# Retention and gated feed-forward on one core: outputs and the new state's transpose in one product of 192 columns

## The chip, the core and the metric

The kernel runs on one core of a Trainium2 chip. The engines of a core work side by side: TensorE (PE) multiplies matrices and writes to PSUM, VectorE (DVE) and ScalarE (ACT) work elementwise on SBUF and PSUM, GpSimd (POOL) works elementwise on SBUF alone in this kernel, and SyncE (SP) issues most of the transfers from and to DRAM. They wait for one another by semaphores. The metric is the device time of one execution in microseconds; the kernel before took 1027.68 us in the median of three runs (1027.46 to 1027.72).

## The reference

Eight batches, eight heads, 576 tokens, 64 channels per head. The first part is retention, that is attention without softmax and with a decay by distance; the second is a feed-forward block on its result.

```python
# q, k, v: (8, 8, 576, 64)
scores = q @ k.T / sqrt(64)
gamma = 1 - 2 ** (-5 - arange(8))                  # one per head
ret = scores * (gamma ** (i - j) if i >= j else 0)
attn = ret @ v
# x: attn as (4608, 512); w_in (512, 2048), w_out (2048, 512)
h = x @ w_in
g = h * erf(softplus(h))
out = g @ w_out
```

q, k, v and the result are float32; w_in and w_out come as float64 and are brought to float32 by the kernel.

## The kernel before

**Attention in pieces.** The 4608 tokens are cut into 36 pieces of 128. A batch has four pieces of 128 tokens and a rest of 64; the rests of two batches make one piece. So pieces 8, 17, 26 and 35 hold two rests, and all others belong to one batch; pieces 0, 4, 9, 13, 18, 22, 27 and 31 begin a batch. Four pieces are one chunk of 512 tokens for the feed-forward part.

The decay is split: the value of token j is weighed with gamma^-j (GpSimd, `weigh_values`), the result of token i with gamma^i, when it is taken out of PSUM. Earlier pieces of the same batch come in by a state, the 64x64 matrix k^T v of each head, summed over the pieces and decayed. Heads lie in pairs: pair p holds heads 2p and 2p+1, one in partitions 0 to 63 and one in 64 to 127 (`heads[e]`).

One piece goes through three stages: `transposes` brings q and k to the channel-by-token layout (by TensorE and ScalarE for early pieces, by VectorE for later ones), `scores` makes q k^T and masks it, and `outputs` makes the result and the new state:

```python
def outputs(i):
    segments = pieces[i]
    t = live.pop(i)
    seen = [(kept[b], r0, n) for b, s0, n, r0 in segments if s0 > 0]
    b, s0, n, _ = segments[0]
    o = [ps_at.tile([P, NP, P], FP32, tag="at", name=f"o{j}") for j in range(2)]
    for p in range(NP):                               # scores times values: L365
        for e in range(2):
            nc.tensor.matmul(
                o[p % 2][heads[(e + p) % 2], p // 2, :],
                lhsT=t["v"][:, 2 * p + e, :],
                rhs=t["sT"][:, e, p, :],
                ...
            )
    for state, r0, m in seen:                         # state times q: L376
        for p in range(NP):
            for e in range(2):
                nc.tensor.matmul(
                    o[p % 2][heads[(e + p) % 2], p // 2, r0 : r0 + m],
                    lhsT=state[heads[e], p, :],
                    rhs=t["qT"][heads[e], p, r0 : r0 + m],
                    ...
                )
    if n == P:                                        # keys times values: L388
        kv = flat(o[0])[:, 2 * P :].rearrange("p (a d) -> p a d", a=NP)
        for p in range(NP):
            for e in range(2):
                nc.tensor.matmul(
                    kv[heads[e], p, :],
                    lhsT=t["k"][:, 2 * p + e, :],
                    rhs=t["v"][:, 2 * p + e, :],
                    ...
                )
    # ... (cut: x's tile, the function scaled)
    scaled(1)                                         # VectorE: out of PSUM, times gamma^i
    if n == P:
        sums = kv
        if s0 > 0:
            sums = att.tile([P, NP, D], FP32, tag="sums", name="sums")
            tt(sums, kv, kept[b], ALU.add)            # VectorE
        # ... (cut: new, a tile)
        (nc.gpsimd if s0 > 0 else nc.vector).tensor_tensor(out=new, in0=sums, in1=gp, op=ALU.mult)
        kept[b] = new
    scaled(0)
    load(i + 3, "kv")
    if i + 1 >= SQUARES:
        weigh_values(i + 1)
```

With (e + p) % 2, the two heads of an odd pair lie in exchanged halves of the result; the order of w_in's rows makes up for it.

**Feed-forward part.** It runs in four passes (g) over groups of the 2048 inner columns, and in each over nine chunks (c). Both matrix products of a chunk are done in the manner of Strassen's method: seven products (`A11`, `A12`, `S2`, `S3`, `S1`, `S4`, `A22`) in place of eight, at the cost of sums of x, of the weights and of the results. One of those products is four matmuls of 256 columns:

```python
def product(self, a, acc, start):
    for j in range(GP):
        for d in range(2):
            nc.tensor.matmul(acc[:, j * TH : (j + 1) * TH],
                lhsT=weights["wa", self.g][:, a, d, j * P : (j + 1) * P],
                rhs=x[self.g, self.c][a][:, d, :], ...)
```

Chunks 0 and 1 of the first pass do the first product without this, in `plain()`: 32 matmuls of 256 columns, which need neither sums of x nor of weights.

**Order.** The program order of all engines is fixed by the kernel: between the products of the feed-forward part, `attend` issues one more stage of the attention, and `round_weights` issues the next step of converting the weights from their double-precision bits to float32. Before the first loads are there, `keep_busy` issues idle products of a tile of ones.

Of the kernel before, what the change touches and what calls it, by code (L numbers as in the profile page):

```python
# [2 lines left out]

# [28 lines left out]
def decays():  # L32
# [7 lines left out]
    out = np.where(np.arange(NP) % 2 == 0, row, np.roll(row, D, axis=0))  # L40
    t = np.arange(P)
    parts = []
    for n in (P, D):
# [3 lines left out]
        gq = out[:, :, None] ** i[None, None, :] / math.sqrt(D)  # L47
# [7 lines left out]
def kernel(  # L55
# [66 lines left out]

    def load_squares(i, name, src):
# [12 lines left out]
    def load_rows(i, name, src, bufs):  # L136
        if name == "q":
            t = raw.tile([P, NP, P * D // SQ], FP32, tag="qs", name="raw_q", bufs=bufs)
            t = t.rearrange("p a x -> p (a x)")[:, : H * D].rearrange("p (h d) -> p h d", h=H)
        else:  # L140
            t = raw.tile([P, H, D], FP32, tag=name, name=f"raw_{name}", bufs=bufs)
# [22 lines left out]
    ones = cpool.tile([P, P], FP32, name="ones")  # L164
    nc.vector.memset(ones, 1.0)
# [26 lines left out]
    def parts():  # L192

        w2 = w_in.rearrange("(e c d) (h f) -> c e d h f", c=n_dc, d=D, h=2)
        for g in range(n_g):
            for dc in range(n_dc):
                a = A11 if dc < 2 else A12
                src = [(heads[(e + dc) % 2], w2[dc, e, :, :, 2 * g * GW : 2 * (g + 1) * GW]) for e in range(2)]

                yield src, "wa", g, a, dc % 2, ["wa"] if g > 0 and dc == n_dc - 1 else []  # L200
            for f in range(2):
                for j in range(GP):
                    ft = f * FH // P + g * GP + j
                    src = [(slice(0, P), w_out[ft * P : (ft + 1) * P, :].rearrange("p (h o) -> p h o", h=2))]
                    sums = (["wb"] if g > 0 else ["wb", "wa"]) if (f, j) == (1, GP - 1) else []
# [97 lines left out]
    kept = {}  # L303
    weighed = set()

# [9 lines left out]
    def transposes(i):  # L315
        t = live[i] = loaded.pop(i)
        if i < SQUARES:
# [23 lines left out]
    def scores(i):  # L341
        t = live[i]
        sT = t["sT"] = att.tile([P, 2, NP, P], FP32, tag="sT", name="sT")
# [10 lines left out]
    def outputs(i):  # L354
        segments = pieces[i]
        t = live.pop(i)
# [3 lines left out]

        b, s0, n, _ = segments[0]
        o = [ps_at.tile([P, NP, P], FP32, tag="at", name=f"o{j}") for j in range(2)]
        for p in range(NP):
            for e in range(2):
                nc.tensor.matmul(  # L365
                    o[p % 2][heads[(e + p) % 2], p // 2, :],
                    lhsT=t["v"][:, 2 * p + e, :],
                    rhs=t["sT"][:, e, p, :],
# [4 lines left out]
        for state, r0, m in seen:  # L373
            for p in range(NP):
                for e in range(2):
                    nc.tensor.matmul(  # L376
                        o[p % 2][heads[(e + p) % 2], p // 2, r0 : r0 + m],
                        lhsT=state[heads[e], p, :],
                        rhs=t["qT"][heads[e], p, r0 : r0 + m],
# [4 lines left out]
        if n == P:  # L384
            kv = flat(o[0])[:, 2 * P :].rearrange("p (a d) -> p a d", a=NP)
# [14 lines left out]
        def scaled(j):  # L400
            to = x[0, c][:, j:NP:2, at : at + P]
            if c < n_ch - 1:
                by = (gq if n == P else gq2)[:, j::2, :].unsqueeze(2).to_broadcast([P, 2, P // n, n])
                dst, got = (y.rearrange("p a (m i) -> p a m i", i=n) for y in (to, o[j][:, :2]))
# [3 lines left out]
            for r0 in range(0, P, n):  # L408
# [3 lines left out]
                    for y in (o[j][:, :2, r0 : r0 + n], (gq if n == P else gq2)[:, j::2, :])  # L412
# [4 lines left out]
        if n == P:  # L417
            sums = kv
            if s0 > 0:
                sums = att.tile([P, NP, D], FP32, tag="sums", name="sums")  # L420
                tt(sums, kv, kept[b], ALU.add)

            if b % 2 == 0 and s0 + P + D == S:
                new = att.tile([P, NP, D], FP32, tag="last", name="last", bufs=1)
            else:
                new = att.tile([P, NP, D], FP32, tag="state", name="state")
# [3 lines left out]
        load(i + 3, "kv")  # L430
# [27 lines left out]
    PLAIN = 2  # L458
# [276 lines left out]
    def keep_busy(n):  # L735
        for _ in range(n):
            nc.tensor.matmul(idle[:, :P], lhsT=ones, rhs=ones, start=True, stop=True)
# [16 lines left out]
    for what in "alkakakawkakakawwaa3awa2aaa5ppppaa5wwppa5ppawappwcppa5ppaaapp5s":  # L754
# [18 lines left out]
    store_x(1)  # L773
    for step, _ in enumerate(firsts[1].plain()):
        if step % 2 == 0:
            attend(min(done[0] + 1, most[0]))
        round_weights(int(step > 1))
        if step == 1:
            firsts[0].softplus()
            firsts[0].erf()  # L780
        elif step == 5:
            firsts[0].multiply()
        elif step == 8:
# [80 lines left out]
```

## Time and profile before

| | |
|---|---|
| time, median of 3 runs | 1027.68 us |
| span of the profiled execution | 1024.0 us |
| granted TensorE clock | 1.000 |
| last attention product | at about 314 us |
| HBM read, written | 117.52 MB, 47.19 MB |

Shares of the engines by stretch of the span, from the busy time of each:

| stretch, us | PE | DVE | ACT | POOL | DMA engines |
|---|---|---|---|---|---|
| 28 to 60 | 97% | 70% | 36% | 25% | 95% |
| 110 to 200 | 100% | 75% | 29% | 20% | 95% |
| 200 to 310 | 100% | 80% | 33% | 25% | 90% |
| 310 to 490 | 100% | 62% | 43% | 11% | 44% |
| 490 to 1024 | 99% | 60% | 39% | 5% | 40% |

A group of the profile is named by its line of the kernel, engine, operation and tiles (`o<-sT,raw_v`: written tile, read tiles), with the part of the array that it uses (`128*64`: 128 rows, 64 columns), partitions by elements, and the count; behind the bar stand the busy time in us, the mean duration of one in ns, and the idle time in front with what ended it. A float32 matmul of the program is two instructions in the trace (for a transpose, one). Line 99 is the helper `tt`, that is all elementwise work of VectorE on two tensors.

### The profile page before, as it was taken

What the parts mean: (1) busy time and instruction counts of PE and PEld (TensorE: products, weight loads), DVE (VectorE), ACT (ScalarE), POOL (GpSimd) and SP (SyncE); (2) the same over time, 40 slices, a digit from 0 to 9 for tenths busy, and PEclk for the clock granted to TensorE, in tenths of its full rate; (3) what the DMA queues carried; (4) which work ended last, traced back from release to release, by engine and by line L of the source; (5) the groups of instructions that cost most, each with busy time, mean ns of one, the idle gap of its engine ahead of it and who ended that gap; (6) DMA issues with size and microseconds to landing.
All of it is one profiled execution on the core that took longest, in us unless ns stands there. A gap on an engine that the chain in (4) does not pass through costs nothing.

```text
span 1024.0 us, 15958 instructions
## 1 busy us (share of the span) xinstructions
PE 1017.6 (99%) x6348; PEld 876.0 (86%) x6348; DVE 667.6 (65%) x1062; ACT 390.2 (38%) x481; POOL 122.6 (12%) x122
## 2 busy tenths in 40 slices
PE   9999999999999999999999999999999999999998
PEld 8787888888888888888888888888888888888887
DVE  3769777976976656656666666666567655555555
ACT  3354134234134444334343444444433333333332
POOL 2143112122312110010001001000100000000000
PEclk9999999999999999999999999999999999999999
DMA  9998989979974354544444345444433333444434
GB/s 200 203 242 175 232 203 223 255 150 253 244 195 150 106 161 145 165 160 154 164 147 158 124 147 162 165 144 144 144 124 124 124 131 127 131 136 131 126 88 119
DMA packets 146986, 165.76 MB, mean 162 GB/s; under 512 B 97376, under 2 KB 121568, under 8 KB 138848
## 3 DMA queue, kind: packets, MB, share of 16 engines
q1 hardware_dynamic: 144832, 163.57, 56.4%
q10 hardware_dynamic: 2080, 1.18, 0.5%
q8 instruction: 50, 0.82, 0.4%
q14 instruction: 24, 0.20, 0.1%
HBM read 117.52 MB, written 47.19 MB: 161 GB/s over the span
## 4 chain that ended last, share of the span: by engine, by line
PE 94%; DMA 3%; DVE 2%; SPq 1%; POOL 1%; issue 0%; ACTq 0%; DVEq 0%; POOLq 0%
PE a L604 24%; PE a L496 23%; PE g L604 12%; PE g L496 12%; PE e L496 6%; PE e L604 6%; PE o L365 3%; PE s L347 3%; PE o L388 2%; DMA raw_k<-in_k_dram 1%; PE o L376 1%; DMA raw_v<-in_v_dram 1%; PE f L668 1%; SPq L147 1%; PE p L550 1%; PE h L668 1%
## 5 line engine op out<-in xcount | busy, mean ns | idle before, releaser
L496 PE MATMUL a<-x,wa 128*128 128x256 f32 x1088 | 258.3, 380 | 0.0
L496 PEld LDWEIGHTS a<-x,wa 128*128 128x128 f32 x1088 | 205.7, 190 | 28.5
L604 PE MATMUL a<-wb,s 128*128 128x256 f32 x840 | 200.0, 381 | 0.0
L604 PEld LDWEIGHTS a<-wb,s 128*128 128x128 f32 x840 | 158.4, 190 | 22.9 <-ACT o L618 0.7
L99 DVE TENSOR_TENSOR t<-g,t 128x512 f32<-128x512 f32 x68 | 47.0, 691 | 151.9 <-ACT t L526 114.1
L496 PE MATMUL g<-x,wa 128*128 128x256 f32 x544 | 129.2, 380 | 0.0
L496 PEld LDWEIGHTS g<-x,wa 128*128 128x128 f32 x544 | 102.8, 190 | 14.4
L99 DVE TENSOR_TENSOR o<-a,o 128x512 f32<-128x512 f32 x104 | 71.4, 687 | 46.4 <-PE a L604 46.4
L521 ACT COPY t<-a 128x512 f32<-128x512 f32 x34 | 19.9, 586 | 188.3 <-PE a L496 188.3
L99 DVE TENSOR_TENSOR t<-t,s 128x1024 f32<-128x1024 f32 x72 | 88.4, 1267 | 0.0
L274 POOL TENSOR_TENSOR wraw<-wraw 128x512 f32<-128x512 f32 x28 | 29.4, 1051 | 438.1 <-DVE wraw L272 184.4
L565 ACT ACTIVATE s<-t 128x1024 f32<-128x1024 f32 x72 | 72.1, 1049 | 24.6 <-DVE t L99 24.5
L99 DVE TENSOR_TENSOR x<-x 128x512 f32<-128x512 f32 x115 | 75.8, 693 | 1.2
L532 ACT COPY t<-a 128x512 f32<-128x512 f32 x34 | 19.9, 586 | 144.4 <-PE a L496 144.4
L569 ACT ACTIVATE s<-s 128x1024 f32<-128x1024 f32 x72 | 72.1, 1049 | 0.4
L604 PE MATMUL g<-wb,s 128*128 128x256 f32 x280 | 66.7, 381 | 0.0
L604 PE MATMUL e<-wb,t 128*128 128x256 f32 x280 | 66.6, 380 | 0.0
L604 PE MATMUL a<-wb,t 128*128 128x256 f32 x280 | 66.6, 380 | 0.0
L604 PE MATMUL g<-wb,t 128*128 128x256 f32 x280 | 66.4, 380 | 0.0
L99 DVE TENSOR_TENSOR sT<-s,cst 128x512 f32<-128x512 f32 x72 | 46.2, 682 | 30.4 <-PE s L347 30.4
L496 PE MATMUL e<-x,wa 128*128 128x256 f32 x272 | 64.8, 381 | 0.0
L99 DVE TENSOR_TENSOR o<-g,o 128x512 f32<-128x512 f32 x70 | 47.9, 684 | 20.9 <-ACT o L618 18.1
(86 smaller groups left out, 1247.1 us busy)
## 6 DMA issues: line engine op xcount, KB each, us to landing
od<-o SPq DMA_DIRECT2D x54, 512.0 KB, 3.3
x<-xd SPq DMA_DIRECT2D x27, 1024.0 KB, 4.8
o<-od SPq DMA_DIRECT2D x27, 1024.0 KB, 5.4
raw_qs<-in_q_dram SPq DMA_DIRECT2D x96, 112.0 KB, 4.4
raw_ks<-in_k_dram SPq DMA_DIRECT2D x84, 112.0 KB, 4.2
xd<-x SPq DMA_DIRECT2D x9, 1024.0 KB, 5.2
raw_v<-in_v_dram SPq DMA_DIRECT2D x64, 128.0 KB, 4.5
wraw<-in_moe_w_in_dram SPq DMA_DIRECT2D x32, 256.0 KB, 5.7
```

The lines of the kernel that those rows point to most:

```text
L99: nc.vector.tensor_tensor(out=out, in0=in0, in1=in1, op=op)
L274: engine.tensor_tensor(out=r_f, in0=high_f, in1=r_f, op=ALU.mult)
L347: nc.tensor.matmul(ps[e][:, p, :], lhsT=t["kT"][heads[e], p, :], rhs=t["qT"][heads[e], p, :], start=True, stop=True)
L365: nc.tensor.matmul(o[p % 2][heads[(e + p) % 2], p // 2, :], lhsT=t["v"][:, 2 * p + e, :], rhs=t["sT"][:, e, p, :], start=(p < 2), stop=(no ...
L388: nc.tensor.matmul(kv[heads[e], p, :], lhsT=t["k"][:, 2 * p + e, :], rhs=t["v"][:, 2 * p + e, :], start=False, stop=(p == NP - 1), skip_gr ...
L496: nc.tensor.matmul(acc[:, j * TH : (j + 1) * TH], lhsT=weights["wa", self.g][:, a, d, j * P : (j + 1) * P], rhs=x[self.g, self.c][a][:, d, :],
L521: nc.scalar.copy(out=self.t1[:, 1], in_=self.a)
L532: nc.scalar.copy(out=self.t2[:, 0], in_=self.a)
L565: nc.scalar.activation(self.s[:, j], t, AF.Softplus)
L569: nc.scalar.activation(self.s[:, j], self.s[:, j], AF.Erf)
L604: nc.tensor.matmul(acc[:, tp, :], lhsT=left[:, j * TH + tp * P : j * TH + (tp + 1) * P], rhs=weights["wb", self.g][:, b, j, :], start=(sta ...
L668: nc.tensor.matmul(acc, lhsT=left[:, j * TH + tp * P : j * TH + (tp + 1) * P], rhs=weights["wb", self.g][:, b, j, :], start=(b in (B11, B2 ...
```

## The change

Five things go together.

1. From piece 13 on, in pieces of one batch, masked scores and keys of a head lie side by side in one tile, `keys`, 128 and 64 columns. One product with the values as the stationary operand gives the outputs in 128 columns and v^T k, the transpose of the new state's share, in 64 more. The separate products of keys and values go for those pieces.
2. That share comes out of PSUM by VectorE's transpose, which turns blocks of 32x32. GpSimd adds and decays; ScalarE puts the off-diagonal blocks of each head in their places (`place_state`).
3. The state is written into a tile `whole`, as a block-diagonal 128x128 matrix for each pair. State times q of both heads of a pair is then one product of 128x128 and not two of 64x64. For this, head e must lie in half e of the result, so (e + p) % 2 becomes e, for all pieces; w_in's rows follow.
4. Keys as rows now live in the tile `keys`; for pieces from 13 on they are loaded for two pieces ahead, where it was three; those of 13 and 14 are loaded at the end of piece 12.
5. Chunk 1 of the first pass does its first product by seven products, like later chunks. The order around it is changed accordingly, and the sums of the weights wa of the first pass are issued earlier.

The tile of ones for the idle products goes; they read `whole`, which is set to zero at first.

```diff
+    BESIDE = 13
+    WIDE = P + D
+    keys = att.tile([P, 3, H * WIDE], FP32, name="keys", bufs=1)
...
+    whole = cpool.tile([P, NP, P], FP32, name="whole")
+    nc.vector.memset(whole, 0.0)
...
+    def place_state():
+        while unplaced:
+            dst, src = unplaced.pop()
+            for e in range(2):
+                for a in range(2):
+                    rows, to = (slice(e * D + x * SQ, e * D + (x + 1) * SQ) for x in (a, 1 - a))
+                    cols = (e * D if dst is whole else 0) + a * SQ
+                    nc.scalar.copy(
+                        out=dst[to, :, cols : cols + SQ], in_=src[rows, :, (1 - a) * SQ : (2 - a) * SQ]
+                    )
...
     def outputs(i):
+        place_state()
+        wide = n == P and i >= BESIDE
         for p in range(NP):
             for e in range(2):
+                h = 2 * p + e
                 nc.tensor.matmul(
-                    o[p % 2][heads[(e + p) % 2], p // 2, :],
-                    lhsT=t["v"][:, 2 * p + e, :],
-                    rhs=t["sT"][:, e, p, :],
+                    o[p % 2][heads[e], p // 2, : WIDE if wide else P],
+                    lhsT=t["v"][:, h, :],
+                    rhs=beside(i)[:, h, :] if wide else t["sT"][:, e, p, :],
...
         for state, r0, m in seen:
             for p in range(NP):
+                dst, by = o[p % 2][:, p // 2, r0 : r0 + m], t["qT"][:, p, r0 : r0 + m]
+                if state is whole and n == P:
+                    nc.tensor.matmul(
+                        dst, lhsT=whole[:, p, :], rhs=by, start=False, stop=(p >= NP - 2), skip_group_check=True
+                    )
+                    continue
                 for e in range(2):
                     nc.tensor.matmul(
-                        o[p % 2][heads[(e + p) % 2], p // 2, r0 : r0 + m],
-                        lhsT=state[heads[e], p, :],
-                        rhs=t["qT"][heads[e], p, r0 : r0 + m],
+                        dst[heads[e]],
+                        lhsT=state[heads[e], p, heads[e] if state is whole else slice(0, D)],
+                        rhs=by[heads[e]],
...
-        if n == P:
+        if n == P and not wide:
             ... (keys times values)
...
+        if wide:
+            sums = att.tile([P, NP, D], FP32, tag="sums", name="sums", bufs=1)
+            for j in (1, 0):
+                nc.vector.transpose(out=sums[:, j::2, :], in_=o[j][:, :, P:WIDE])
+            new = att.tile([P, NP, D], FP32, tag="state", name="state", bufs=1)
+            if s0 > 0:
+                nc.gpsimd.tensor_tensor(out=sums, in0=sums, in1=squares_kept[0], op=ALU.add)
+            nc.gpsimd.tensor_tensor(out=new, in0=sums, in1=gp, op=ALU.mult)
+            squares_kept[0] = new
+            ... (places: the last state of an even batch as before, else the two diagonal blocks of whole)
+            for rows, dst in places:
+                nc.gpsimd.tensor_tensor(out=dst, in0=sums[rows], in1=gp[rows], op=ALU.mult)
+            unplaced.append((kept[b], new))
...
-        load(i + 3, "kv")
+        load(i + 3, "kv" if i + 3 < BESIDE else "v")
+        for j in range(i + 1 if i + 1 == BESIDE else i + 2, i + 3):
+            if BESIDE <= j < len(pieces) and i + 1 >= BESIDE and len(pieces[j]) == 1:
+                load_rows(j, "k", k, None)
...
-    PLAIN = 2
+    PLAIN = 1
...
     attend(after_chunk(1))
-    store_x(1)
-    for step, _ in enumerate(firsts[1].plain()):
-        if step % 2 == 0:
+    attend(done[0] + 1)
+    operands_x(0, 1)
+    f = firsts[1]
+    for step, _ in enumerate(chain(f.first(), f.middle(), f.last())):
+        if step > 0:
             attend(min(done[0] + 1, most[0]))
-        round_weights(int(step > 1))
-        if step == 1:
+        round_weights((0, 2, 2, 2, 2, 3, 3)[step])
+        if step == 0:
             firsts[0].softplus()
             firsts[0].erf()
-        elif step == 5:
+        elif step == 2:
             firsts[0].multiply()
-        elif step == 8:
+        elif step == 4:
             firsts[0].sums()
     seconds[0].begin()
-    run(seconds[0].first(), (2, 2))
-    firsts[1].softplus()
+    run(seconds[0].first())
```

## The prediction

> **What bounds the kernel now.** I read the head of the page first, then the groups of TensorE by shape, then the order of time of one piece of attention, then single stretches of the span, then the queue that issues the loads.
>
> The head says that TensorE is the bound, and that nothing else is near it over the whole span:
>
> ```profile
> span 1024.0 us, 15958 instructions
> PE 1017.6 (99%) x6348; PEld 876.0 (86%) x6348; DVE 667.6 (65%) x1062; ACT 390.2 (38%) x481; POOL 122.6 (12%) x122
> ```
>
> 99% busy alone doesn't prove it (a matmul's end is modelled, and matmuls overlap), so I count starts. In the long products two instructions start 216 ns apart (a 256-column product of the program is two instructions, a `product` of four is eight: 1.73 us, as the chain of waits has it). They follow each other at that spacing from 90 us to the end with no two starts more than 0.33 us apart. So the time is the sum of what TensorE streams, plus what it loses when it changes tiling, plus a few waits in the first 90 us. A change here is worth what it changes in that sum.
>
> The attention's groups, by shape:
>
> ```profile
> L347 PE MATMUL s<-qT,kT 64*128 64x128 f32 x576 | 41.8, 285 | 0.6 <-ACT kT L338 0.3 <-DVE qT L326 0.3
> L365 PE MATMUL o<-sT,raw_v 128*64 128x128 f32 x576 | 41.1, 279 | 0.4
> L388 PE MATMUL o<-raw_v,raw_k 128*64 128x64 f32 x512 | 21.5, 226 | 0.0
> L376 PE MATMUL o<-qT,state 64*64 64x128 f32 x384 | 16.0, 282 | 0.0
> ```
>
> The last one is the surprise: it has two thirds of L365's instructions but takes 39% of its time. The order of time of one piece says why (columns: start, duration of the group, engine, line, what):
>
> ```profile
> 200.28 1.09 PE L365 MATMUL o<-sT,raw_v 128*64 128x128 f32 x16
> 201.30 0.67 PE L376 MATMUL o<-qT,state 64*64 64x128 f32 x16
> 201.90 0.69 PE L388 MATMUL o<-raw_v,raw_k 128*64 128x64 f32 x16
> 202.51 1.99 PE L604 MATMUL e<-wb,t 128*128 128x256 f32 x8
> 204.44 1.16 PE L347 MATMUL s<-qT,kT 64*128 64x128 f32 x16
> 205.53 1.99 PE L496 MATMUL a<-x,wa 128*128 128x256 f32 x8
> 207.36 1.89 PE L496 MATMUL g<-x,wa 128*128 128x256 f32 x8
> ```
>
> Single starts inside these groups: L365 comes in twos, each two 109 ns after the last; L388 in twos, 58 ns apart; L376 in *fours*, 109 ns apart. L376 runs four at once because the line puts head e of pair p into half (e+p)%2 of the output, so that two pairs use four different 64x64 quarters of the array. The eight instructions of a long product take 1.93 us behind such a group and 1.73 behind another product.
>
> **What the Trainium skill says.** "TensorEngine Tiling (Array Packing)", Key Properties: changing the tiling mode drains TensorE, and separate tiles load and multiply in parallel. The trace agrees with both, and gives the price: the step from L365's last start to L376's first is 0.20 us instead of 0.109, and its first step inside is 0.16 instead of 0.109; together 0.145 us for the change, 0.14 for that back to 128*64, 0.20 for that to 128*128, 0.14 for that out of 128*128. "Perfetto Trace Analysis", Identifying the Most-Contended Engine: matmul busy is no good measure of TensorE. Agreed; hence starts. "VectorE: DVE Perf Modes", The three transpose paths: its transpose turns 32x32 blocks, each by itself. No run so far shows it on this tile, but the change's four ScalarE copies per piece, of the two off-diagonal blocks of each head, follow from it.
>
> **The change part by part.**
>
> *The wide product* (20 pieces: 13 to 16, 18 to 25, 27 to 34). A step of two at 128 columns is 109 ns, one instruction of 256 columns 216, so at 192 columns I take the middle, 162 ns. In 15 of them a state is also read.
> - Before: 0.144 (into 128*64) + 8 x 0.109 + 0.145 + 4 x 0.109 + 0.14 + 8 x 0.058 + 0.198 (out) = 2.40; read directly, the last start before to the second start after, less two steps of 216: 2.43 us.
> - After: the state is a block-diagonal 128x128, four products, eight instructions. Such an instruction at 128 columns takes 112 ns (the warm idle products of L737 start 112 apart). 0.144 + 8 x 0.162 + 0.198 + 8 x 0.112 = 2.54 us. Two changes of tiling are saved (0.28 us); but the state costs 0.90 instead of 0.44, and 64 more columns cost 0.43 instead of 0.46. So +0.11 each, 15 x 0.11 = +1.6 us.
> - The five without a state: 0.144 + 0.872 + 0.464 + 0.198 = 1.68 before, 0.144 + 1.30 + 0.198 = 1.64 after: -0.2 us in all.
>
> *Heads no longer crossed.* The block-diagonal state needs head e in half e, so (e+p)%2 becomes e everywhere, also where the state is still read as 64x64. Two tiles are then in use, not four: eight steps instead of four. A piece of 128 with a state: +4 x 0.109 = +0.44 us. There are nine before piece 13; 5, 6, 7, 10, 11, 12 lie where TensorE is the bound: +2.6 us. Pieces 1, 2, 3 (16 to 28 us) stand ahead of two short waits on loads, 0.29 and 0.39 us near 33 us, which would take up most of it: +0.4 us. The four short pieces (8, 17, 26, 35) read two states at 64 columns, 16 steps of 58 ns instead of 8: +0.47 each, +1.9 us.
>
> *Second chunk by seven products.* 32 products of 256 columns become 28: eight instructions of 216 ns less, -1.73 us.
>
> TensorE's own sum: 1.6 - 0.2 + 2.6 + 0.4 + 1.9 - 1.73 = **+4.6 us**.
>
> *Waits that I expect to be added.* First, VectorE around the second chunk. It has little to spare there (columns: stretch, busy us and instructions of PE, PEld, DVE, ACT, POOL, then clock, DMA share, GB/s):
>
> ```profile
> 60.00:90.00 30.00, 29.64 (x274) 23.98 (x274) 23.27 (x41) 17.24 (x22) 11.04 (x10) 1.00 0.98 226
> 90.00:110.00 20.00, 20.00 (x195) 16.11 (x195) 19.45 (x30) 5.63 (x7) 4.72 (x6) 1.00 0.94 231
> ```
>
> The seven products add four sums of x (3.5 us for the four of the next chunk, at 99.5 us) and three additions of 0.69: 5.6 us, while the four sums of wa (2.8 us) move to before 60 us. The order of instructions also puts ScalarE's 6.8 us of softplus and erf (with two table loads of 1.28) right behind the chunk's first copy, and VectorE's next step of rounding behind ScalarE's. TensorE then waits for the last of the wb to be rounded by GpSimd, or for masked scores: +1.0 us net of the 0.8 us it waits there now (0.27 for the transpose of q at 80.8 us, and 0.5 at 86.85, where L365 lasts 1.61 us and not 1.09).
>
> Second, the keys of pieces 13 and 14. They were fetched three pieces ahead and are now asked for at the end of piece 12, because their place in the shared tile is free only then. The load queue of before, at that place:
>
> ```profile
> 110.33 0.38 SPq L709 DMA_DIRECT2D od<-o  x1
> 110.80 1.38 SPq L147 DMA_DIRECT2D raw_k<-in_k_dram  x2
> 112.28 1.16 SPq L147 DMA_DIRECT2D raw_v<-in_v_dram  x2
> ```
>
> These are piece 15's loads, which stand behind others in the queue; keys of 13 in that slot would be issued near 112 and land 4.5 us later (the median of raw_k), at 116.5, while piece 13's outputs start at 114.1. The three key loads left out ahead of it make the queue a little shorter: +1.5 us, once.
>
> Third, the new state's way: two VectorE transposes, three or four GpSimd steps of about 0.61 us (the 128x256 product of before has 613 ns) where there was one, then four ScalarE copies, which I put at 0.24 us each from 0.58 for 512 columns and 1.05 for 1024. Now 6.6 us lie between the end of one piece's outputs and the start of the next, GpSimd's state starts 0.6 to 2.4 us after that end, and the weighing of the next values (1.04 to 1.5 us) comes behind it. 2.4 + 0.4 + 2.45 + 1.2 = 6.4 us at worst: just in time. Only in piece 15 do the copies stand behind the two softplus instructions with just one product and the wide one ahead of the state: +0.7 us. The first memset is four times as large, and the idle products wait for it: +0.2 us.
>
> Waits: 1.0 + 1.5 + 0.7 + 0.2 = +3.4 us. In all 1027.7 + 4.6 + 3.4 = **1035.7 us**.
>
> **The rivals.** (a) The product pays as meant: eight products of kv fewer in a piece, each with its own weight load, and fewer drains are worth more than my steps say, the head crossing costs nothing, and only the 1.7 us of the second chunk and a little more remain: 1023 to 1026 us. For it: PEld has "issue" gaps in these groups. Against: these gaps lie beside running matmuls, and the fours of L376 are plain in the trace. (b) The state's way is too long: the GpSimd chain of up to 6.4 us against 6.6 goes over in every second piece, by a microsecond, or the copies wait behind table loads: 20 pieces x 0.5 to 1 us: 1042 to 1050 us. For it: the chain has twice as many hands. Against: in 9 of the 15 pieces GpSimd starts within 1.3 us of the end. (c) The loads: the share of the DMA engines is 0.90 to 0.95 up to 310 us, and the later keys could make several pieces wait, not one: 1038 to 1042. Against: bytes and number of loads are the same, and later keys still come a whole piece early.
>
> **Range and chances.** The +4.6 is counted from starts and I trust it within 1.5; the waits are between 0 and 8. I choose 1035.5 us, 1030 to 1042. Two per cent are 20.6 us; faster by that would need 26 us less than TensorE's sum allows (1%), slower by that needs rival b at its full size (6%).
>
> **What would show it.** Right: the state lines with 64*64 at two starts per 109 ns, the wide group at about 1.4 us and L421 at about 1.0 us per piece, the long products 1.73 behind L421 and not 1.93; 32 plain products fewer and 28 of the sevens more; one hole on TensorE in front of piece 13 with a key load as its cause, one in front of L421 with ScalarE. Wrong: fours on the diagonal, a wide step well under 162 ns, a 128x128 step far from 112 ns, or TensorE waiting for GpSimd in most pieces.

## The result, and the profile after

| | before | after |
|---|---|---|
| time, median of 4 runs each on one chip | 1027.57 us (1027.05 to 1027.72) | 1041.32 us (1039.74 to 1041.87) |
| span of the profiled execution | 1024.0 us | 1040.1 us |
| granted TensorE clock in it | 1.000 | 0.998 |

The ratio is 1.0132, with a 95% interval of 1.0115 to 1.015: the change costs 1.3%, 13.75 us by the medians. The profiled executions lie 16.1 us apart. The one of after is among the longest of its four, and the one of before, 1024.0 us, is shorter than most: beside the experiments below, before's spans are 1023.7 to 1027.3 us. The accounts below are of the profiled executions and so come out some 2 us higher than the medians.

The head of the page of after, to be laid beside that of before:

```profile
span 1040.1 us, 15262 instructions
...
PE 1026.7 (99%) x5900; PEld 882.5 (85%) x5900; DVE 684.0 (66%) x1086; ACT 414.2 (40%) x561; POOL 169.6 (16%) x180
```

448 instructions fewer on TensorE, and its busy time is 9.1 us longer: fewer products are not less time. GpSimd has 47 us more to do, in 58 more instructions.

TensorE's attention groups of after, by shape (they answer L365, L376 and L388 of before):

```profile
L409 PE MATMUL o<-keys,raw_v 128*64 128x192 f32 x320 | 32.3, 335 | 3.9 <-DMA keys<-in_k_dram 2.4 <-POOL raw_v L352 1.0 <-issue 0.5
L421 PE MATMUL o<-qT,whole 128*128 128x128 f32 x120 | 17.4, 288 | 0.9 <-ACT whole L341 0.9
L426 PE MATMUL o<-qT,state 64*64 64x128 f32 x144 | 9.8, 275 | 0.0
```

L426 is the state still read as 64x64: 144 instructions in 9.8 us, where before 384 took 16.0. That is 68 ns for each instruction where it was 42: the fours have become twos. And the wide product has idle time in front of it, which no attention group of before had in that amount.

The order of time around piece 13 (the first wide product, without a state) and piece 14 (with one):

```profile
116.00 1.89 PE L566 MATMUL g<-x,wa 128*128 128x256 f32 x8
120.29 2.54 PE L409 MATMUL o<-keys,raw_v 128*64 128x192 f32 x16 [2.40 <-DMA keys<-in_k_dram]
122.76 3.15 PE L566 MATMUL a<-x,wa 128*128 128x256 f32 x8
...
130.58 1.52 PE L409 MATMUL o<-keys,raw_v 128*64 128x192 f32 x16
132.03 1.16 PE L421 MATMUL o<-qT,whole 128*128 128x128 f32 x8
```

The undisturbed piece 14 is as the prediction had it: 1.45 us from the wide product's start to the state's, 1.0 us for the state. The hole in front of piece 13 was foreseen too. What was not foreseen stands behind it: the same wide product takes 2.54 us instead of 1.52, and the product after it 3.15 us, where such a product took 1.99 before. About 0.2 us of this is a second stop inside the wide product, from 120.47 to 120.86 us: the second load of these keys lands at 120.72. In the product after it, starts are 427 ns apart. TensorE's clock is halved for a while, as single stretches show (columns: stretch, busy us and instructions of PE, PEld, DVE, ACT, POOL, then clock, DMA share, GB/s):

```profile
122.00:124.00 2.00, 2.00 (x7) 1.28 (x5) 1.13 (x4) 0.00 (x0) 0.12 (x1) 0.50 1.04 240
124.00:126.00 2.00, 2.00 (x8) 1.37 (x9) 0.02 (x1) 0.06 (x1) 1.85 (x4) 0.72 1.16 210
```

The waits of TensorE, with total, count and longest in us (wb are the rounded weights of the second product of a chunk):

```profile
PE o L409 <- DMA keys<-in_k_dram: 2.4, 1, 2.4
PE o L409 <- POOL raw_v L352: 1.6, 3, 0.7
PE e L674 <- POOL wb L300: 1.6, 1, 1.6
...
PE o L421 <- ACT whole L341: 0.9, 1, 0.9
```

None of the four is there in the profile of before. The first of them comes once, in front of piece 13. The second is the chain of GpSimd that the prediction called "just in time": L352 is the weighing of the next piece's values, and it comes behind the making of the state. GpSimd's own order of time at the end of piece 34, and TensorE's start of piece 35:

```profile
323.22 0.73 POOL L474 TENSOR_TENSOR sums<-sums,state 128x256 f32<-128x256 f32 x1 [3.93 <-DVE sums L471]
324.03 0.94 POOL L475 TENSOR_TENSOR state<-sums,cst 128x256 f32<-128x256 f32 x1
324.93 1.29 POOL L484 TENSOR_TENSOR whole<-sums,cst 64x256 f32<-64x256 f32 x2
326.30 1.10 POOL L352 TENSOR_TENSOR raw_v<-raw_v,cst 128x512 f32<-128x512 f32 x1
```

```profile
327.46 1.16 PE L409 MATMUL o<-keys,raw_v 128*64 128x128 f32 x16 [0.69 <-POOL raw_v L352]
```

4.2 us of GpSimd in a row, and TensorE starts 0.06 us after its end.

### The profile page after: what moved, and what is told of

Same layout as the page of the kernel before. It is cut to its first block, busy times and chain, and to the rows that moved or that the text cites. A ratio compares the mean times of both kernels' runs of the same rounds, so it can differ in the third digit from the quotient of the medians.

```text
span 1040.1 us, 15262 instructions
## 1 busy us (share of the span) xinstructions
PE 1026.7 (99%) x5900; PEld 882.5 (85%) x5900; DVE 684.0 (66%) x1086; ACT 414.2 (40%) x561; POOL 169.6 (16%) x180
## 4 chain that ended last, share of the span: by engine, by line
PE 82%; DMA 7%; DVE 4%; SPq 3%; issue 2%; POOL 1%; ACT 1%; DVEq 0%; POOLq 0%
PE a L566 21%; PE a L674 21%; PE g L566 11%; PE g L674 10%; PE e L674 5%; PE e L566 5%; DMA raw_qs<-in_q_dram 2%; PE o L409 2%; DMA keys<-in_k_dram 2%; PE s L387 1%; SPq L172 1%; DMA raw_v<-in_v_dram 1%; SPq L154 1%; PE o L426 1%; DMA raw_ks<-in_k_dram 1%
## 5 line engine op out<-in xcount | busy, mean ns | idle before, releaser
L566 PE MATMUL a<-x,wa 128*128 128x256 f32 x1120 | 267.0, 381 | 0.0
L566 PEld LDWEIGHTS a<-x,wa 128*128 128x128 f32 x1120 | 212.3, 191 | 30.0 <-issue 0.5
L566 PE MATMUL g<-x,wa 128*128 128x256 f32 x560 | 132.9, 380 | 0.0
L566 PEld LDWEIGHTS g<-x,wa 128*128 128x128 f32 x560 | 105.7, 190 | 14.9 <-issue 0.3
L99 DVE TENSOR_TENSOR x<-x 128x512 f32<-128x512 f32 x116 | 79.8, 721 | 1.2
L99 DVE TENSOR_TENSOR keys<-s,cst 128x512 f32<-128x512 f32 x72 | 46.2, 682 | 24.1 <-PE s L387 24.1
## 6 DMA issues: line engine op xcount, KB each, us to landing
x<-xd SPq DMA_DIRECT2D x27, 1024.0 KB, 4.8
o<-od SPq DMA_DIRECT2D x27, 1024.0 KB, 5.2
xd<-x SPq DMA_DIRECT2D x9, 1024.0 KB, 5.2
```

What stands on the lines that cost most here:

```text
L99: nc.vector.tensor_tensor(out=out, in0=in0, in1=in1, op=op)
L566: nc.tensor.matmul(acc[:, j * TH : (j + 1) * TH], lhsT=weights["wa", self.g][:, a, d, j * P : (j + 1) * P], rhs=x[self.g, self.c][a][:, d, :],
```

## The experiments

Fourteen kernels in all are compared: before, after, and the twelve below. Ratios are to the kernel before, run beside each on the same chip; its median there was between 1026.9 and 1027.5 us.

### 1. Only the crossing of heads removed, from the kernel before

```diff
-                    o[p % 2][heads[(e + p) % 2], p // 2, :],
+                    o[p % 2][heads[e], p // 2, :],
...
-                        o[p % 2][heads[(e + p) % 2], p // 2, r0 : r0 + m],
+                        o[p % 2][heads[e], p // 2, r0 : r0 + m],
```

(the rows of w_in and the constants follow)

> The kernel before with one thing changed: head e of every pair lies in half e of the result, so the state products use two 64x64 tiles and not four. Theory of counted starts: 21 pieces with a state at +0.42 us, the three earliest mostly hidden (+0.4 in all), four short pieces at +0.46: +11 us, 1038 to 1039 us, with the state group (L376) in twos 109 ns apart and no new wait. Rival, that the changed kernel lost its time to waits and the tiles are free: within 1 us of before.

Measured: 1036.3 us, ratio 1.0095 (1.0077 to 1.0112), 9.4 us over before, and so some 1.6 us less than the 11 that the theory counted; the profiled spans come nearer. Every piece with a state is longer by 0.42 us, each short piece by 0.45; no wait is new. 21 such pieces in the stretch where TensorE is the bound, and four short ones, give 21 x 0.42 + 4 x 0.45 = 10.6 us; the profiled spans differ by 10.5. The group of the state shows it, with the same 384 instructions that took 16.0 us:

```profile
L375 PE MATMUL o<-qT,state 64*64 64x128 f32 x384 | 26.2, 276 | 0.0
```

So the arrangement of before was worth 1%, and it isn't visible in the number of instructions or in the mean of one.

### 2. Only the seven products of the second chunk, in the kernel before

```diff
-    PLAIN = 2
+    PLAIN = 1
...
+    for step, _ in enumerate(chain(f.first(), f.middle(), f.last())):
...
+        round_weights((0, 2, 2, 2, 2, 3, 3)[step])
```

> The kernel before with only the second chunk's first product done by seven products, with the order around it as in the changed kernel. Theory: 1.73 us less on TensorE, given back by waits there (a wait of about 1.6 us on the rounding of wb, and masked scores): 1027 to 1028.5 us. Rival, that it pays as counted and the waits come from the heads' longer state products: 1025.5 to 1026.3 us.

Measured: 1027.62 us against 1026.9, ratio 1.0005 (0.9997 to 1.0014): nothing gained from 1.73 us less of products. TensorE now waits for the last rounded part of wb in the middle of a product:

```profile
PE e L605 <- POOL wb L276: 1.6, 1, 1.6
```

### 3. After, with the second chunk plain again

The opposite edit in the kernel after.

> The changed kernel with the second chunk plain again, all else kept. Theory as for the seven products alone: about 1041 us, no better and no worse than the changed kernel by more than 1 us, and no wait of TensorE for GpSimd's wb. Rival, that the seven products pay: 1043 us.

Measured: 1040.76 us, ratio 1.0135 (1.0117 to 1.0153), the same as after. The wait for wb is gone, and with it the gain: this part of the change is neutral in both surroundings, here within the interval of some 1.8 us on either side. (In this profile the hole in front of piece 13 is 3.39 us, and the clock is halved for 6.8 us.)

### 4. After, with the keys of piece 13 asked for one piece earlier

```diff
-        return keys[:, i % 3, :].rearrange("p (h x) -> p h x", h=H)
+        return keys[:, (i + 1) % 3, :].rearrange("p (h x) -> p h x", h=H)
...
-        for j in range(i + 1 if i + 1 == BESIDE else i + 2, i + 3):
+        for j in range(i + 2, i + 3):
```

The three places in the tile are dealt out in another turn, so that the one for piece 13 is free a piece earlier.

> The changed kernel with the keys' places rotated by one, so that piece 13's keys can be loaded at the end of piece 11 and 14's at the end of 12, like all later ones. Theory: the 2.4 us wait in front of piece 13 goes, and with it the 2.2 us that the slower clock costs behind it: 1036 to 1037.5 us, clock 1.000. Rival, that the loads as a whole are too late: the wait moves to piece 14 or 15 and the time stays at 1039 or more.

Measured: 1036.23 us, ratio 1.0094 (1.0079 to 1.0109), 5.1 us less than after, or 4.4 when each is set against before on its own chip (9.3 and 13.75 us over it): the wait of 2.4 and what stands behind it were worth about twice the wait. Piece 13 in the order of time:

```profile
117.92 1.52 PE L409 MATMUL o<-keys,raw_v 128*64 128x192 f32 x16
119.37 1.99 PE L566 MATMUL a<-x,wa 128*128 128x256 f32 x8
```

### 5. In addition, the next values weighed ahead of the state

```diff
         if wide:
+            weigh_values(i + 1)
...
-        if i + 1 >= SQUARES:
+        if i + 1 >= SQUARES and not wide:
             weigh_values(i + 1)
```

> The kernel with early keys (1036.2 us), and in wide pieces GpSimd weighs the next piece's values before it makes the state, not after. Theory: TensorE's waits for weighed values in pieces 17, 19, 26, 27, 30, 34 and 35 (about 3.9 us between starts in the changed kernel's trace) go: 1032 to 1034 us. Rival: the state then comes 1.04 us later for everybody and the same time is lost in front of the state products (L421 behind ScalarE's copies): 1036 us.

Measured: 1034.65 us, ratio 1.0072 (1.0055 to 1.0089). About half a microsecond above what was expected. The waits for `raw_v` are gone, pieces 17, 26, 30, 34 and 35 take the time of undisturbed ones, and the profiled span falls from 1034.9 to 1032.9: the order of GpSimd's work was the cause of those delays. Three others stay that it can't touch: ScalarE's copies in piece 15 (1.1 us), VectorE's mask in 19 (0.33) and a delay of 0.47 in 27, whose second load of keys lands at 244.77 us; TensorE goes on at 244.86.

### 6. After, with the block-diagonal state read as two 64x64 for each pair

```diff
-                if state is whole and n == P:
+                if False:
```

> The changed kernel, but the state in the block-diagonal tile is read as two 64x64 blocks for each pair, in all pieces; the wide product stays. Theory: 0.872 us and two more changes of tiling for 0.896: +0.12 us in each of 15 pieces, +1.8 us, 1042.5 to 1043.5 us. Rival, that the zeros of the 128x128 block are the waste to be saved: 1036 to 1040 us.

Measured: 1042.82 us, ratio 1.0147 (1.0131 to 1.0162), as expected; the difference from after is within the noise of the medians, and the profile decides: an undisturbed piece costs 0.23 us over before and not 0.11. So the block-diagonal product is right *once the heads are uncrossed*: four full products beat eight quarter ones in twos, by 0.12 us. It only loses to the fours of before.

### 7 and 8. The wide product with the heads crossed, as before

If the fours cost least, the wide product can keep them: v^T k then lies in crossed halves, from which VectorE's transposes take it, and `whole` is an ordinary state tile read by 64x64 products.

```diff
-            for j in (1, 0):
-                nc.vector.transpose(out=sums[:, j::2, :], in_=o[j][:, :, P:WIDE])
+            for e in range(2):
+                nc.vector.transpose(out=sums[heads[e], 1::2, :], in_=o[1][heads[1 - e], :, P:WIDE])
+            nc.vector.transpose(out=sums[:, 0::2, :], in_=o[0][:, :, P:WIDE])
```

(of the edit only the transposes are shown; those of 4 and 5 are in it too; the second chunk is plain in 7, by seven products in 8)

> The kernel before (heads crossed, second chunk plain) with the wide product from piece 13 on, the state kept as 64x64 blocks and read in fours, keys early and values weighed first; VectorE's transpose of odd pairs writes to the other half. Theory: 0.144 + 8 x 0.162 + 0.145 + 0.436 + 0.20 = 2.22 us for 2.40 in 15 pieces: -2.7 us, -0.2 in the five others, and up to 1 us of new waits: 1024 to 1025.5 us where before has 1026.9. Rival: the wide product itself is the loss, or its longer chain to the state: no faster than before.

> As the last, with the second chunk by seven products too. Theory: these pay back what they cost, within 1 us of the last kernel. Rival: with fewer products on TensorE it gains 1.7 us more.

Measured: 1034.07 us, ratio 1.0067 (1.0052 to 1.0082), and 1034.83 us, ratio 1.007 (1.0055 to 1.0085). That the two agree was foreseen; that neither beats before was not, by 9 us. The undisturbed pieces do what was counted: with a state there are 2.68 us from the last start ahead of the piece's group to the second start behind it, where before has 2.87, so 0.19 us less each; without one 0.04 less. The profile of 7 has new waits in their place:

```profile
PE o L410 <- DMA keys<-in_k_dram: 3.5, 4, 1.4
...
PE o L410 <- POOL state L473: 1.0, 1, 1.0
```

The second line names GpSimd, but this product (of piece 35) reads `keys` and `raw_v` and not the state. VectorE's first mask of `keys` ends at 319.68 us and the product starts at 319.78: what came last is VectorE.

The keys' loads are asked for two pieces ahead (as in after), where before did it three ahead. Their issue for piece 25, in the load queue of 7 and then of the kernel before:

```profile
221.38 1.16 SPq L173 DMA_DIRECT2D keys<-in_k_dram  x2
```

```profile
203.87 0.94 SPq L147 DMA_DIRECT2D raw_k<-in_k_dram  x2
```

The queue issues in order and is late: the request placed at the end of piece 23, near 206 us, leaves it 15 us later. From 209.50 to 221.34 us the queue issues the twenty loads of the short piece 26, which stand ahead of it. "Two pieces ahead" is a distance in the program, and at this load it is none in time.

### 9. As 7, with the keys asked for three pieces ahead, and ahead of the values

```diff
-        load(i + 3, "kv" if i + 3 < BESIDE else "v")
+        if i + 3 < BESIDE:
+            load(i + 3, "k")
...
-        for j in range(i + 2, i + 3):
-            if BESIDE <= j < len(pieces) and len(pieces[j]) == 1:
+        for j in {BESIDE - 2: [BESIDE], BESIDE - 1: [BESIDE + 1, BESIDE + 2]}.get(i, [i + 3] if i >= BESIDE else []):
+            if j < len(pieces) and len(pieces[j]) == 1:
                 load_rows(j, "k", k, None)
+        load(i + 3, "v")
```

> crossed_plain with one thing changed: the keys are asked for as soon as their place is free, those of piece 15 and later at the end of the outputs three pieces ahead (two ahead in crossed_plain), those of 13 at the end of piece 11, 14 and 15 at the end of 12, and ahead of the values in the queue, as in the kernel before. Theory: crossed_plain missed its 1024 to 1025.5 by some 9 us because its keys stood behind other loads in SyncE's queue, which runs ten us late: TensorE waited for keys in four pieces, and later waits are partly their consequence. So the waits for keys go (none over 0.3 us), and about half to all of the 7 us of the pieces 18 to 35 with them: 1026 to 1030 us. Rival: the chain of the new state (VectorE's two transposes out of PSUM, GpSimd's steps, ScalarE's copies) is what is late, and the keys only end the wait last: then other waits take their place and the time stays at 1032 to 1035 us.

Measured: 1029.36 us (20 runs) against 1027.31, ratio 1.0019 (1.0012 to 1.0026). 4.7 us less than 7, or 4.5 when each is set against before on its own chip; all waits of L410 for keys are gone. This is in the range of the theory; the keys of piece 25 are now issued at 205.41 us. It still doesn't beat before. Aligned with before piece by piece, the undisturbed pieces bring their 0.19 and 0.04 us, and what it loses against them stands in few places: 0.97 in piece 15 (ScalarE's copies), 0.5 at piece 22, 0.25 at 26, 1.6 behind piece 30, 1.8 at pieces 34 and 35 (the expectation of experiment 12 puts these last two at 1.4 and 2.6). In front of piece 35 it is VectorE's mask of `keys` again: it ends at 314.13 us, the product starts at 314.23. Behind piece 30 it is VectorE's transposes of k:

```profile
PE s L388 <- DVE kT L367: 1.4, 2, 1.2
```

VectorE's order of time ahead of that place, and GpSimd's:

```profile
259.20 3.52 DVE L100 TENSOR_TENSOR x<-x 128x512 f32<-128x512 f32 x4
```

```profile
260.20 1.37 POOL L353 TENSOR_TENSOR raw_v<-raw_v,cst 128x512 f32<-128x512 f32 x1 [5.15 <-DMA raw_v<-in_v_dram]
```

and the same four sums of x in the kernel before, where GpSimd stood still beside them:

```profile
258.73 2.59 DVE L99 TENSOR_TENSOR x<-x 128x512 f32<-128x512 f32 x4
```

The sums last 0.93 us longer beside GpSimd's weighing (0.85 of it in the third of the four), the transposes of v^T k (0.64 and 0.32 us) take 0.96 us where the sum with the state took 0.41, and VectorE, which has no break in this stretch, comes to the next transposes at 270.47 us where before does at 268.10: 2.4 us later, of which it had 0.5 ahead of these sums.

### 10. The seven products with the rounding spread otherwise

```diff
-        round_weights((0, 2, 2, 2, 2, 3, 3)[step])
+        round_weights((2, 3, 3, 2, 2, 1, 1)[step])
```

(in the kernel of experiment 2; the lines below are waits of scores, of a product of the feed-forward part and of a transpose of k)

> sevens with the steps of the rounding spread otherwise over the seven products of the second chunk: 2, 3, 3, 2, 2, 1, 1 and not 0, 2, 2, 2, 2, 3, 3. Theory: the 1.73 us of TensorE that the seven products save were given back by one wait of 1.6 us for the last rounded part of wb, which is late because VectorE and GpSimd come to it behind softplus and erf of ScalarE. With the rounding earlier that wait is under 0.3 us, and the kernel takes 1.0 to 1.7 us less than the kernel before on the same chip. Rival: VectorE has no time left in the stretch from 60 to 110 us, and whatever is put first, something else (masked scores, sums of x) comes as much later: no gain, within 0.5 us of the kernel before.

Measured: 1030.48 us against 1027.31, ratio 1.0034 (1.0021 to 1.0048). The theory falls, and by more than its rival said: the wait for wb goes, and others come, 4.4 us in three places between 78 and 88 us.

```profile
PE s L348 <- DVE qT L327: 1.8, 1, 1.8
PE g L497 <- DVE t L100: 1.3, 1, 1.3
PE pt_k L333 <- DVE x L100: 1.3, 1, 1.3
```

All three are VectorE's. The stretch has no room on VectorE for four more sums of x and three additions, in this order or in that of the change. Whether some third order fits was not tried.

### 11. The hole alone, in the kernel before

```diff
-        load(i + 3, "kv")
+        load(i + 3, "v" if i == 10 else "kv")
+        if i == 12:
+            (loaded.get(13) or live[13])["k"] = load_rows(13, "k", k, 4)
```

> The kernel before with one load moved: the keys of piece 13 are asked for at the end of piece 12, behind the loads of piece 15, and not at the end of piece 10. No instruction of TensorE changes. Theory: a hole of 2 us or more in TensorE brings the clock down behind it. The keys land near 117 to 118.5 us and are wanted at 115.0, so TensorE stands still for 2 to 3.5 us in front of piece 13's keys times values, and the matmuls of the next 5 us start 427 ns apart and not 216, which adds 2 us more: 4 to 6 us over the kernel before in all (1031 to 1033), and the mean granted clock is under 1. Rival: the clock drop in the changed kernel had another cause (its wide product, or its state), and here the time grows by the hole alone: 2 to 3.5 us (1029.3 to 1030.8), clock 1.000, and the next product takes 1.9 to 2.0 us.

Measured: 1031.88 us against 1027.01, ratio 1.0051 (1.0037 to 1.0065): 4.9 us, the time that the theory expected. The profiled execution, however, shows the rival's picture:

```profile
118.20 1.13 PE L388 MATMUL o<-raw_v,raw_k 128*64 128x64 f32 x16 [2.27 <-DMA raw_k<-in_k_dram]
119.26 1.99 PE L498 MATMUL a<-x,wa 128*128 128x256 f32 x8
```

The product behind the hole takes its usual 1.99 us, and the clock of that execution is 1.000; the delay from this place is 2.9 us, and the execution loses 0.8 us ahead of it and 1.9 in short waits behind piece 26. The four other executions have a mean clock of 0.997 to 0.998, about what 3.4 us at half clock make of 1030 (1 - 1.7/1030 = 0.998). They took 1031.16 to 1033.17 us, and the profiled one 1031.41. So a hole of this length is sometimes followed by the half clock and sometimes not (the last section shows on what it depends in the profiles), and this run doesn't fix the clock's own cost: the 4.9 us are the hole, other waits and, it seems, the clock, in shares that stay open.

### 12. The wide product only where it met no wait

From 9, with the wide product from piece 18 on and not in pieces 30 and 34:

```diff
-    BESIDE = 13
+    BESIDE = 18
+    NARROW = (30, 34)
...
-        wide = n == P and i >= BESIDE
+        wide = n == P and i >= BESIDE and i not in NARROW
```

> crossed_three with the wide product only where it met no wait: from piece 18 on (13 before), and not in pieces 30 and 34, the last ones of a batch, whose states are read by piece 35. Counted gain on TensorE: 8 pieces with a state at 0.19 us, 3 without at 0.04: 1.6 us. crossed_three lost about 1 us in piece 15 behind ScalarE's copies, 1.4 behind piece 30 and 2.6 at pieces 34 and 35, which go; it also lost 0.6 at piece 22, 0.25 at piece 26, and 0.7 before piece 13, which stay. Theory: 0 to 0.7 us over the kernel before on the same chip less its spread, that is within 1 us of it on either side. Rival: VectorE and GpSimd slow each other down wherever the state's steps are added, and the losses only move to other pieces: 1.5 us or more over the kernel before.

Measured: 1029.76 us against 1027.01, ratio 1.0021 (1.001 to 1.0033); three of seven executions took 1027.1 to 1027.4 us, four 1029.8 to 1030.6. By its median this is the rival's case; the profiled execution is one of the longer four. Pieces 18 to 27 gain what was counted, less the known losses at 22 and 26. This execution is 1.5 us late before the first wide product (0.9 of it a wait for keys at 68.3 us), and 3.2 us are lost in pieces 28 to 30:

```profile
PE o L411 <- POOL whole L478: 1.4, 1, 1.4
PE s L389 <- DVE kT L368: 1.2, 2, 1.0
```

The first line names GpSimd, but here too the product reads `keys` and `raw_v` alone: VectorE's mask of `keys` ends at 268.94 us, the product starts at 269.04. Both waits end with VectorE.

None of the twelve beats the kernel before.

## Why the prediction was right, and where it wasn't

1035.5 us was predicted, 1041.32 measured: in the range of 1030 to 1042, near its upper edge, and within 2% as given 93%. By its own terms, in us, with what the profile of after shows when each piece is aligned with the same piece of before (the waits of the second chunk are what the other terms leave of pieces 5 to 12, and the 0.6 us of the first pieces are not sure to be the heads': the kernels of 7 and 9, with heads crossed, lose 0.55 and 0.71 there too):

| term | predicted | measured in the profiles |
|---|---|---|
| wide product with a state, 15 pieces | +1.6 | 15 x 0.11 = +1.65 |
| wide product without, 5 pieces | -0.2 | 5 x -0.04 = -0.2 |
| heads uncrossed, pieces 5 to 12 | +2.6 | 6 x 0.42 = +2.5 |
| heads uncrossed, short pieces | +1.9 | 4 x 0.45 = +1.8 |
| pieces 1 to 3, and the first memset | +0.4 + 0.2 | +0.6 together |
| second chunk, products | -1.73 | -1.73 |
| second chunk, waits for VectorE and wb | +1.0 | +1.9 |
| keys of piece 13, the hole | +1.5 | +2.4 |
| half clock and second load of keys behind it | not counted | +2.2 |
| ScalarE's copies, piece 15 | +0.7 | +1.0 |
| GpSimd's weighing, "just in time" | 0 | +2.5 |
| keys of piece 27; VectorE's mask in piece 19 | not counted | +1.1 + 0.3 |
| sum | +8.0 | +16.0 |

In this account TensorE's own sum is 4.4 us for 4.6 predicted, and the waits are 11.6 us (some 9 by the medians) where 3.4 were predicted and "between 0 and 8" allowed. So the half of the forecast that was counted from starts held, and the half that was estimated did not. That the total still lies in its range owes something to luck: the range left room for 1.5 us more of TensorE's own, which did not come, and the waits used it.

**TensorE's own sum** was right to 0.2 us: the step of 162 ns at 192 columns, the 112 ns at 128x128, the prices of a change of tiling and the twos in place of fours all held. Experiments 1, 6 and 7 confirm them one at a time. Rival (a), fewer products and so less time, has nothing left: with the heads crossed the product is worth 0.19 us in a piece with a state, and after gave up 0.30 in each such piece (0.11 over before in place of 0.19 under it), and 0.42 to 0.45 in ten others, to have it in a block-diagonal form.

**"Just in time"** is the step that failed. It set 6.4 us of work against 6.6 of room for the state's way and took that for zero. That sum ends with ScalarE's copies and leaves out the weighing of the next values, which the same sentence names with 1.04 to 1.5 us; by the prediction's own figures the weighing would end after 2.4 + 0.4 + 2.45 + 1.04 to 1.5 = 6.3 to 6.75 us. And what came late was not the state but this weighing, which stands behind the state in GpSimd's order: in pieces 30 and 34 by 0.55 and 0.67 us, in the short pieces 17, 26 and 35 by 0.12, 0.31 and 0.83; together 2.5 us, of which experiment 5 gave back about 2. Rival (b) named the chain and expected it in every second piece; it was in five of 23. The chain was also longer than steps of 0.61 us make it: the addition of the old state takes 0.72 to 0.73 us in all fifteen pieces, and beside VectorE a multiplication stretches to 0.94 and the weighing to 2.02. And a margin of 0.2 us is none where the start of the chain scatters by 1.8.

**The keys.** The hole was foreseen in its place and cause. Its size, 2.4 us where 1.5 was expected, comes from the queue: the keys are four issues, those of 13 and 14, and the loads of raw_v went out ahead of them from 114.62 us on, so that the keys' issues begin at 116.02 and not near 112:

```profile
116.02 2.75 SPq L172 DMA_DIRECT2D keys<-in_k_dram  x4
```

What stands behind the hole was in no term, and was nearly as large. The half clock can be at most 1.7 of these 2.2 us (half of 3.41 us), and the second load of keys about 0.2; the rest is not split up. Removing all of it gave 4.4 to 5.1 us back (experiment 4). One of the four executions of after has a mean clock of 1.000 and not 0.998; its span is 1036.8 us, those of the others are 1039.0 to 1040.1.

**The second chunk.** It was expected to be worth 1.73 - 1.0; it is worth nothing, as experiments 2 and 3 show from both sides. VectorE was busy for 28.05 us of the 30 from 60 to 90 us, and for 23.27 before:

```profile
60.00:90.00 30.00, 28.34 (x254) 23.23 (x253) 28.05 (x45) 17.79 (x24) 12.23 (x10) 1.00 0.87 210
```

**Rival (c)**, several pieces that wait for keys, holds for two in after. Besides 13 it is piece 27, which the profile puts down to no wait: TensorE stops for 0.8 us between the first product and the second. The second of the two key loads was issued at 245.16 us and landed at 249.93; TensorE goes on at 250.02. In experiment 7, where TensorE ran ahead faster, it was four pieces, and restoring three pieces of lead, with the keys ahead of the values, brought 4.5 to 4.7 us. So the prediction's "later keys still come a whole piece early" is true in the program and not in the queue.

Open stays how much of the 2 to 3 us that experiments 9 and 12 lose to before is due to GpSimd's two more steps for each state, and how much to VectorE's longer transposes. The largest waits in both end with VectorE, but the two shares were read from one place in one profile; no run takes them away.

## What to carry over

Count small products in starts and in the parts of the array that they use at once: eight quarter products that run four at a time cost less than four that use the whole array, so an arrangement that looks odd, such as heads laid crosswise, may be what makes an already tuned kernel fast, and a change that has to give it up starts with that debt. When work moves to an engine that is mostly idle, what counts is not its share of busy time but the place of the new work in its order, ahead of what TensorE waits for next. And a load's lead is measured from its issue on the queue, not from its line in the program; in a kernel that is bound by TensorE a late load is paid for again if the clock goes down behind it.

## What the runs showed of the hardware

**The clock.** A hole of 2.78 us between two starts on TensorE (2.36 us in experiment 8, 2.69 in 6, 3.39 in 3) was followed by a stretch at half clock: starts 427 ns apart instead of 216, in after from 121.7 to 125.1 us. In the profile of experiment 11 a hole of 2.55 us was not. The traces show on what this depends. The stretches that they note at one clock are whole multiples of 3.413 us (34, 1 and 268 of them in after; 64, 1 and 236 in experiment 8), so the clock is set window by window. In the windows just ahead of the four drops TensorE is idle for 2.05 us (after), 2.06 (3), 2.13 (6) and 2.42 (8) of the 3.41. The windows at the end of the fourteen profiles, where the matmuls run out, fit in: those idle for 2.06 us or more have the half clock behind them. None that is idle for 1.94 us or less has it, with one exception: in experiment 3 the window after the drop is idle for 0.95 us only, and the next one is at half clock all the same. In experiment 11 a boundary between two windows, at 117.6 us, cuts the hole into 1.67 and 0.72 us of idle time. So in these profiles it is where a hole falls among the windows that decides, and not its length alone. (Ends of matmuls are modelled, so these idle times are good to a tenth or so.) The Trainium skill, "TensorE: Matmul & The Clock Gate", in What's actually happening, says that the clock follows activity in windows of about 3.4 us that run freely, whatever the kernel does. The multiples of 3.413 us agree with that. That it takes an idle window of 3.4 us, as the page has it, does not agree: here about 2 us within one window were enough.

**VectorE and GpSimd.** Where both work on two SBUF tensors, both can slow down: GpSimd's weighing of 128x512 goes from 1.04 to 2.02 us (pieces 30 and 34 of after), VectorE's four sums of x from 2.59 to 3.52 us in experiment 9. "GPSIMD Engine Reference", Specifications, says that GpSimd's interfaces to SBUF are shared with VectorE, and that VectorE's instructions with two SBUF inputs contend for them. The trace agrees and gives the size. So work moved to GpSimd isn't free for VectorE.
